# Experts' weight splits on VectorE in halves, narrowed pieces stored one piece later, float64 loads two ahead

## The chip, the core and the metric

The kernel runs on one core of a Trainium2 chip. A core has TensorE (PE in the profile; PEld is its weight load), VectorE (DVE), ScalarE (ACT), GpSimd (POOL) and SyncE (SP), which here issues most of the DMAs. Each engine works through its own queue in order and waits on semaphores for the others. The metric is the device time of one execution in microseconds, lower is better.

## The reference

Three stages follow each other, in float32.

```python
# attention: B=4, H=8, S=768, D=48
for t in range(S):
    cur = einsum('bhd,bhe->bhde', u[None] * kt, vt)
    y[:, :, t] = einsum('bhd,bhde->bhe', rt, state + cur)
    state = w[None, :, :, None] * state + einsum('bhd,bhe->bhde', kt, vt)
# experts: x of 3072 tokens x 384, 8 experts of 1024 hidden units, one expert for each token
expert_idx = argmax(x @ w_gate, axis=1)          # and its softmax weight gate_w
out[mask] = gate_w[mask, None] * (maximum(x[mask] @ w1[e], 0) @ w2[e])
# second layer: 2048 hidden units
h = x @ w_in
out = where(h > 0, h, exp(minimum(h, 0)) - 1) @ w_out
```

`w_in` and `w_out` of the second layer arrive as float64, since they are divided by a float64 scalar.

## The kernel before

**Attention** (`attention`, up to about 180 us) works in six chunks of 128 positions. In its last chunk the routing finds out which tokens go to which expert, and the first weights are already loaded and split.

**The experts' jobs.** `JOBS` lists nine jobs: the expert with the most tokens in two jobs of 256 slots (jobs 0 and 1), then the other seven with 448, 432, 416, 408, 408, 392 and 384 slots (jobs 2 to 8). A job has eight steps `f` of 128 hidden units. `step` gives TensorE a first group of nine matmuls (`layer1`, L757: three parts of 128 rows, and for each the products weight x data, weight x data rest, weight rest x data), which ends in `psl`; ScalarE makes `h` from it (L761) and VectorE the rest of `h` (L762). The second group (`layer2_columns`, L789, nine matmuls into `acc`) of a step comes LAG = 2 steps later, behind the first group of step f + 2. In steps 5 to 7 of a job `turn` transposes the next job's rows (L737), ScalarE copies them (L738) and VectorE takes the rest (L739, `xT`).

**The second layer** has six groups of 512 tokens (the code counts them as jobs 9 to 14) with 16 steps each: L757 again, then L766 on ScalarE, L767 and L768 on VectorE, L769 on ScalarE and L770 on VectorE, and twelve matmuls of 384 columns (L928). `take` (L747 on ScalarE, L748 on VectorE) splits the group's inputs. At the end GpSimd scatters the output rows.

**The weights** come in 40 chunks of 128 x 1536 float32 (768 KB): four for each of the eight experts, in their order, and eight for the second layer. `Stream.load` (L650) issues a load on SP's queue into `raw`, which has two buffers. `Stream.split` rounds it on ScalarE to a form that TensorE takes in one pass (L657, into one of four `wc` buffers; the last four chunks of the second layer have four buffers of their own) and subtracts that from the raw chunk (L659), on GpSimd except for chunks 2 and 3, which VectorE takes. `Stream.ahead` is called ahead of a step: at every even step it splits the chunk that is used two chunks later, and loads run one chunk ahead of the splits. A load waits for the subtraction that read its buffer last; the copy on ScalarE waits for its load and for the last matmuls that used its `wc` buffer.

**The narrowing** (`narrow_all`) turns the second layer's float64 weights, taken as bits, into float32 in DRAM (`w2f`), from where the last eight chunks are loaded. It is a generator with 16 pieces of 128 x 768: a load of 768 KB (`load_64`, L837, into `r64` with two buffers), five instructions on VectorE (L852, L855, L859, L862, L866) through the tiles `f` and `sg` with one buffer each, and a store of 384 KB on SP's queue (L867). It is called once in each step of jobs 1 to 8 and once more in steps 2, 4 and 6, eleven times a job, between `turn` and `step`; each call runs to the next `yield`, one instruction. `overflow_plan` (L962 to L1028) is spread over the steps of jobs 1 and 2 in the same way.

**GpSimd** also issues the gathers of the jobs' rows (L715, `xg`, two buffers) and the scatters of the slots (L67, `xi`).

The order of the instructions on each engine is that of the program (the schedule is written by hand). `order` (from L425) sorts the experts with small VectorE instructions.

Of the kernel before, what the change touches and what calls it, by code (L numbers as in the profile page):

```python
# [7 lines left out]
F32 = mybir.dt.float32  # L8
# [3 lines left out]
U32 = mybir.dt.uint32  # L12
ACTF = mybir.ActivationFunctionType
ALU = mybir.AluOpType
# [50 lines left out]
def scatter(tc, nc, apart, key, **kw):  # L65
    """no two scatters under one key write the same row"""
    ins = nc.gpsimd.indirect_dma_start(**kw).ins  # L67
    tc.declare_no_dep(ins, group=key, reason="rows of different tokens")
    tc.add_to_no_dep_group(key, ins)
    nc.gpsimd.memset(apart, 0.0)  # L70


def attention(tc, g, ctx, rkT, kv, wT, uT, wg):
    nc = tc.nc
    con = ctx.enter_context(tc.tile_pool(name="a_con", bufs=1))
    ld = ctx.enter_context(tc.tile_pool(name="a_ld", bufs=2))
    # what the last chunk no longer needs lies where weights will
    rk_b = [g.stream.wc.tile([128, 3, 2, B, C], F32, tag="wc", name=f"rkb{i}") for i in range(2)]
# [34 lines left out]
    def warm(n):  # L113
        """keeps the tensor engine's clock up where it would wait"""
        ps = p_m.tile([128, 512], F32, tag="m", name="psw")
        for _ in range(n):
            nc.tensor.matmul(ps, zero[:, 0:128], zero, start=True, stop=True, skip_group_check=True)
# [8 lines left out]

    # powers: ex[i] = w^(i-64), er[i] = w^(64-i); an inverse is taken at each power of two
    ex = con.tile([128, NP, 129], F32, name="ex")
# [9 lines left out]
    def grow(eng, up, down, step):  # L138
        """up[64 + j] and down[64 - j], j = 1 .. 64, from the powers step(i) = (2^i)-th"""
        for i in range(7):  # L140
            n = 1 << i
            m = min(n, 65 - n)
            for t, o, at in ((up, 64, 64 + n), (down, 65 - m, 65 - n - m)):
                if t is not None:
                    eng.tensor_tensor(out=t[:, :, at:at + m], in0=t[:, :, o:o + m],
                                      in1=step(i).to_broadcast([128, NP, m]), op=ALU.mult)

    nc.vector.tensor_copy(out=ex[:, :, 65:66], in_=w_sb.unsqueeze(2))
    for i in range(1, 7):
        n = 1 << i  # L150
# [45 lines left out]
    def pk_rows():  # L196
        """row form of the key powers, times w^128"""
        pks = wk.tile([128, NP, C], F32, tag="ot0", name="pks")
        nc.vector.tensor_tensor(out=pks, in0=pk, in1=w128.unsqueeze(2).to_broadcast([128, NP, C]), op=ALU.mult)
        ps = p_t.tile([128, NP, 128], F32, tag="t", name="pst")  # L200
        for p in range(NP):
            nc.tensor.transpose(ps[:, p, :], pks[:, p, :], g.ident)
        nc.scalar.copy(out=pkr, in_=ps.rearrange("s p (h d) -> s p h d", h=2)[:, :, :, 0:D])
# [22 lines left out]
    def state(c, q):  # L226
        """pairs 2q and 2q+1: the state at the start of chunk c + 1"""
        kr, v = kr_t[c], v_t[c]
# [110 lines left out]
    def rows(c, b, spare=False):  # L339
        """rows of x for a block of 128 tokens, times their gate: it is positive, so that relu lets it through"""  # L340
        if b == 0:
            x = xp.tile([128, B, ROW], F32, tag="x", name="x")
            nc.scalar.copy(out=x[:, :, TID], in_=tid[:, c, :])
            x_t[c] = x
        pool, tag = (p_m, "m") if spare else (p_t, "t")
        ps = pool.tile([128, NP, 128], F32, tag=tag, name="pst")
        for p in range(NP):
            nc.tensor.transpose(ps[:, p, :], o_t[c, p][:, b, :], g.ident)
        xv = x_t[c][:, b, 0:DM].rearrange("t (p h d) -> t p h d", p=NP, h=2)
        pv = ps.rearrange("t p (h d) -> t p h d", h=2)[:, :, :, 0:D]  # L350
        gate = gate_t[c][:, b:b + 1]
        nc.scalar.activation(out=xv, in_=pv, func=ACTF.Copy, scale=gate)
# [51 lines left out]
    def counts():  # L404
        """tells the experts apart by the tokens they have so far"""
        ps = p_m.tile([128, E], F32, tag="m", name="psc")
# [7 lines left out]
    def leader():  # L414
        """the expert with the most tokens of the first 2048: 256 or more, which fill the first job's slots"""
        key = counts()
# [7 lines left out]
    def order():  # L424
        """the experts after the leader, by the tokens they have so far"""  # L425
        key = counts()
# [14 lines left out]
    def place(c):  # L441
        """the rows in the order of the tokens, and each slot's row"""
        x, si = x_t[c], si_t.pop(c)
# [7 lines left out]
    def blank():  # L451
        """row 0 is what a slot without a token takes; its id is one that no scatter takes"""
        z = wk.tile([128, ROW], F32, tag="ot0", name="blank")
# [172 lines left out]
class Stream:  # L626
    """chunks of weights, 256 hidden units each: first the experts' in their order, then those of the second layer;
    split into a part that the tensor engine takes in one pass and the rest"""

# [9 lines left out]
    def which(self, p):  # L639
        """the expert at place p of the order"""  # L640
        if p not in self.expert:
# [12 lines left out]
    def split(self, i):  # L654
        w = self.pool(i).tile([128, 2, 1536], F32R, tag="wc", name="wc")
        r = self.loaded.pop(i)
        self.nc.scalar.copy(out=w[:, 0], in_=r)  # L657
        eng = self.nc.vector if i in (2, 3) else self.nc.gpsimd
        eng.tensor_tensor(out=w[:, 1], in0=r, in1=w[:, 0].bitcast(F32), op=ALU.subtract)  # L659
        self.ready[i] = w  # L660
        self.n_split = i + 1

    def ahead(self, n):
        """splits the chunks below n; loads run one ahead"""
        while self.n_split < min(n, self.n):
# [7 lines left out]
class Jobs:  # L673
    """the experts' slots in jobs of up to 512, then the second layer's tokens in groups of 512"""

# [25 lines left out]
    def load_i(self, u):  # L701
        """where the rows of the job's slots lie"""
        p, at, n = JOBS[u]
# [16 lines left out]
    def note(self, u):  # L720
        """the tokens of the job's slots, in the order that the second layer takes them in"""
        nc, g, (p, at, n) = self.nc, self.g, JOBS[u]
# [50 lines left out]
    def finish(self, u, k):  # L773
        """an expert's output to its columns; the next expert's overwrite those of empty slots"""
        nc, (p, at, n) = self.nc, JOBS[u]
# [37 lines left out]
def experts(tc, g, ctx, wpk2, out):  # L813
    nc = tc.nc
    stream, jobs = g.stream, g.jobs
    bp = ctx.enter_context(tc.tile_pool(name="m_b", bufs=1))
    # x of the second layer, columns in the order of the experts
    jobs.mid = mid = [bp.tile([128, N + WIDTH[1]], F32, name=f"mid{k}") for k in range(3)]
# [15 lines left out]
    def load_64(n):  # L834
        q, at = halves[n]
        r = dp.tile([128, 768], wpk2.dtype, tag="r64", name="r64", bufs=2)
        nc.sync.dma_start(out=r, in_=wpk2[0, q, :, at])  # L837
        return r

    def narrow_all():  # L840
        """float64 bits to the nearest float32, kept in DRAM for the second layer; one instruction at a time"""
        for _ in range(5):
            yield
        r = load_64(0)
        for _ in range(2):
            yield
        for n, (q, at) in enumerate(halves):
            v = r.bitcast(U32).rearrange("p (n t) -> p n t", t=2)
            lo, hi = v[:, :, 0], v[:, :, 1]
            r = load_64(n + 1) if n + 1 < len(halves) else None  # L850
            f = dp.tile([128, 768], U32, tag="f", name="f")
            nc.vector.tensor_scalar(out=f, in0=hi, scalar1=3, scalar2=0x3FFFFFF8, op0=ALU.logical_shift_left,  # L852
# [3 lines left out]
                                           op1=ALU.bitwise_or)  # L856
            yield
            t = dp.tile([128, 768], U32, tag="sg", name="sg")
            nc.vector.tensor_scalar(out=t, in0=f, scalar1=0xFF800000, scalar2=None, op0=ALU.bitwise_and)  # L859
# [6 lines left out]
            nc.vector.tensor_tensor(out=w, in0=w, in1=tail, op=ALU.add)  # L866
            nc.sync.dma_start(out=g.w2f[0, q, :, at], in_=w)  # L867
            yield

    narrowing = narrow_all() if wpk2.dtype != F32 else iter(())  # L870

    def clear():
        """columns that stay empty where an expert has more tokens than slots"""
        n = (N + WIDTH[1] - CAP) // 64
# [84 lines left out]
def overflow_plan(nc, g, pool, psum):  # L959
    """where each expert's tokens go between the layers; those beyond its slots, in items of 112 ranks"""  # L960
    cp = psum.tile([128, E], F32, tag="m", name="cp")
# [46 lines left out]
    yield  # L1008
    # each item's expert's width: the first's and the steps from there
    grow = pool.tile([128, E], F32, name="grow")  # L1010
# [20 lines left out]
def overflow(tc, g, wpk, out):  # L1031
    """both layers for the tokens beyond an expert's slots, one item after another"""
    nc = tc.nc
# [154 lines left out]
```

## Time and profile before

| | us |
|---|---|
| median of 3 runs (902.67 to 910.98) | 903.71 |
| span of the profiled execution, first to last instruction | 900.5 |
| TensorE busy in it | 803.0 |
| VectorE busy | 562.5 |
| ScalarE busy | 295.2 |
| GpSimd busy | 306.3 |

For the profiled execution the profile gives the span alone; the median of the runs is 3.2 us longer. The profile's numbers are of that one execution. A row of the timeline is: start, duration, engine, line, operation, output<-inputs, count, and in brackets the idle time of the engine just before and what ended it. A row of the waits is: who waited for whom, us in total, times, longest. A row of a group has the busy time and mean duration in ns, and then the idle time before. A row of one line's instructions has the shortest, median and longest duration in ns.

### The profile page before, as it was taken

How to read it: one execution, taken by the hardware profiler on the slowest of the kernel's cores; microseconds unless marked ns; L12 is line 12 of the kernel's file. 1: busy time of each engine (PE TensorE's matmuls, PEld its weight loads, DVE VectorE, ACT ScalarE, POOL GpSimd, SP SyncE). 2: the span in 40 equal slices, each digit the busy share in tenths (PEclk: the TensorE clock that was granted, in tenths of full speed). 3: DMA queues.
4: the chain of work that ended last, by engine and by line, in shares of the span. 5: the costliest groups of instructions: out<-in, count | busy, mean ns of one | idle time of the engine just before them, and what ended most of it. 6: DMA issues, size and time to landing. Idle time of an engine off the chain costs nothing. (4 is left out here: it accounts for less than half of the span.)

```text
span 900.5 us, 12702 instructions
## 1 busy us (share of the span) xinstructions
PE 803.0 (89%) x4960; PEld 708.1 (79%) x4962; DVE 562.5 (62%) x875; ACT 295.2 (33%) x485; POOL 306.3 (34%) x259
## 2 busy tenths in 40 slices
PE   6577877976879986999899999999999999999994
PEld 3455665766878985999897779999999999999993
DVE  8989999762586828686776774444444544444441
ACT  3111220243553432444344433333333333333221
POOL 7837337263365637375453331001001001001001
PEclk7879988998999989999999999999999999999998
DMA  9336563184876596597562200000000000001001
GB/s 347 126 129 107 169 153 42 40 158 96 197 188 155 214 198 174 153 254 164 197 211 93 101 1 22 15 1 27 10 0 30 7 1 36 1 1 36 1 0 38
DMA packets 31242, 87.54 MB, mean 97 GB/s; under 512 B 11582, under 2 KB 15182, under 8 KB 31178
## 3 DMA queue, kind: packets, MB, share of 16 engines
q1 hardware_dynamic: 26218, 76.57, 31.0%
q0 software_dynamic: 4672, 9.98, 4.4%
q8 instruction: 41, 0.67, 0.4%
q14 instruction: 23, 0.19, 0.1%
q10 hardware_dynamic: 288, 0.13, 0.1%
HBM read 70.67 MB, written 15.99 MB: 96 GB/s over the span
## 5 line engine op out<-in xcount | busy, mean ns | idle before, releaser
L757 PE MATMUL psl<-xT,wc 128*128 128x512 f32 (+6 forms) x1368 | 323.0, 380 | 8.7 <-DVE xT L739 8.7
L757 PEld LDWEIGHTS psl<-xT,wc 128*128 128x128 f32 x1368 | 254.9, 190 | 41.0 <-DVE xT L739 10.0
L928 PE MATMUL acc<-wc,h 128*128 128x384 f32 x1152 | 220.1, 338 | 4.0 <-ACT h L769 3.1
L928 PEld LDWEIGHTS acc<-wc,h 128*128 128x128 f32 x1152 | 204.1, 188 | 16.0 <-ACT h L769 5.7
L659 POOL TENSOR_TENSOR wc<-raw,wc 128x1536 fp32r<-128x1536 f32 x38 | 135.8, 3575 | 140.4 <-ACT wc L657 140.3
L67 POOL DMA_INDIRECT out_dram<-y,idT x24 | 24.7, 1031 | 331.8 <-ACT y L936 326.8
L789 PE MATMUL acc<-h,wc 128*128 128x408 f32 (+6 forms) x576 | 120.6, 352 | 13.4 <-DVE h L762 13.1
L767 DVE TENSOR_SCALAR ex<-ex 128x512 f32<-128x512 f32 x96 | 49.5, 516 | 125.3 <-ACT ex L766 125.3
L789 PEld LDWEIGHTS acc<-h,wc 128*128 128x128 f32 x576 | 104.7, 195 | 19.6 <-DVE h L762 17.6
L770 DVE TENSOR_TENSOR h<-ex,h 128x512 fp32r<-128x512 f32 x96 | 66.5, 693 | 65.9 <-ACT h L769 65.2
L769 ACT CAST h<-ex 128x512 fp32r<-128x512 f32 x96 | 59.6, 620 | 135.2 <-DVE ex L768 135.2
L766 ACT ACTIVATE ex<-psl 128x512 f32<-128x512 f32 x96 | 57.4, 597 | 131.3 <-PE psl L757 122.4
L657 ACT CAST wc<-raw 128x1536 fp32r<-128x1536 f32 x40 | 59.2, 1480 | 69.8 <-DMA raw<-in_wpk_dram 39.9
L768 DVE TENSOR_TENSOR ex<-ex,psl 128x512 f32<-128x512 f32 x96 | 66.0, 688 | 3.4
L852 DVE TENSOR_SCALAR f<-r 128x768 uint32<-128x768 uint32 x16 | 30.4, 1900 | 45.7 <-DMA w2f<-f 33.0
L761 ACT ACTIVATE h<-psl 128x408 fp32r<-128x408 f32 (+6 forms) x64 | 31.7, 499 | 58.3 <-PE psl L757 57.5
L67 POOL DMA_INDIRECT xi<-pos,si x24 | 25.9, 1080 | 71.4 <-DVE acc L401 67.1
L277 PE MATMUL psc<-rt,kt 64*128 64x128 f32 x384 | 34.5, 309 | 17.4 <-DVE a L287 15.1
L277 PEld LDWEIGHTS psc<-rt,kt 64*128 64x128 f32 x384 | 28.5, 207 | 26.8 <-DVE a L287 16.1
L762 DVE SCALAR_TENSOR_TENSOR h<-psl,h 128x408 fp32r<-128x408 f32 (+6 forms) x64 | 35.7, 559 | 21.3 <-ACT h L761 21.3
L315 ACT COPY ot<-pso 128x512 f32<-128x512 f32 x24 | 14.1, 586 | 88.3 <-PE pso L311 54.7
L169 DVE TENSOR_TENSOR kt<-rkb,er 128x512 f32<-128x512 f32 x14 | 41.5, 2972 | 0.3
(175 smaller groups left out, 798.2 us busy)
## 6 DMA issues: line engine op xcount, KB each, us to landing
raw<-in_wpk_dram SPq DMA_DIRECT2D x32, 768.0 KB
rkb<-in_rkT_dram SPq DMA_DIRECT2D x24, 512.0 KB
r<-in_wpk_dram SPq DMA_DIRECT2D x16, 768.0 KB
w2f<-f SPq DMA_DIRECT2D x16, 384.0 KB
raw<-w2f SPq DMA_DIRECT2D x8, 768.0 KB
xl<-x SPq DMA_DIRECT2D x6, 770.0 KB
v<-in_kv_dram SPq DMA_DIRECT2D x6, 768.0 KB
kb<-in_kv_dram SPq DMA_DIRECT2D x5, 768.0 KB
```

The costliest lines, as they stand in the source:

```text
L67: ins = nc.gpsimd.indirect_dma_start(**kw).ins
L277: nc.tensor.matmul(ps[hf][:, b, :], kt[r0:r0 + 64, b, :], rt[r0:r0 + 64, b, :], start=True, stop=True, skip_group_check=True)
L657: self.nc.scalar.copy(out=w[:, 0], in_=r)
L659: eng.tensor_tensor(out=w[:, 1], in0=r, in1=w[:, 0].bitcast(F32), op=ALU.subtract)
L757: nc.tensor.matmul(ps, self.w1(i, a, k, fi), xT[:, b, k], start=(m == 0), stop=(m == 8))
L766: nc.scalar.activation(out=ex, in_=ps, func=ACTF.Exp)
L767: nc.vector.tensor_scalar(out=ex, in0=ex, scalar1=1.0, scalar2=-1.0, op0=ALU.min, op1=ALU.add)
L768: nc.vector.tensor_tensor(out=ex, in0=ex, in1=ps, op=ALU.max)
L769: nc.scalar.copy(out=h[:, 0], in_=ex)
L770: nc.vector.tensor_tensor(out=h[:, 1], in0=ex, in1=h[:, 0].bitcast(F32), op=ALU.subtract)
L789: nc.tensor.matmul(self.acc[u][k], w[:, a, 128 * k:128 * k + 128], h[:, b], start=(f == 0 and m == 0), stop=(f == 7 and m == 2))
L928: nc.tensor.matmul(acc, h[:, a, 128 * j:128 * j + 128], jobs.w2(i, b, fi), start=(f == 0 and m == 0), stop=(f == 15 and m == 2))
```

## The change

All subtractions of `split` run on VectorE, each as two halves of 768 columns (the first holds the weights of the first group, the second those of the second). The narrowing has two buffers for `f`; the store of a piece is issued behind the second instruction of the next piece, and the last one at the end. `r64` has three buffers; two loads are issued at the start, two calls sooner than the first was, and then each piece issues the load of the piece two ahead. The first piece's first instruction stays at the same call. Comments and docstrings are removed.

```diff
@@ Stream.split
         self.nc.scalar.copy(out=w[:, 0], in_=r)
-        eng = self.nc.vector if i in (2, 3) else self.nc.gpsimd
-        eng.tensor_tensor(out=w[:, 1], in0=r, in1=w[:, 0].bitcast(F32), op=ALU.subtract)
+        for k in range(2):
+            at = slice(768 * k, 768 * k + 768)
+            self.nc.vector.tensor_tensor(out=w[:, 1, at], in0=r[:, at], in1=w[:, 0, at].bitcast(F32), op=ALU.subtract)
@@ load_64
-        r = dp.tile([128, 768], wpk2.dtype, tag="r64", name="r64", bufs=2)
+        r = dp.tile([128, 768], wpk2.dtype, tag="r64", name="r64", bufs=3)
@@ narrow_all
-        for _ in range(5):
+        for _ in range(3):
             yield
-        r = load_64(0)
-        for _ in range(2):
+        rs = [load_64(0), load_64(1)]
+        for _ in range(4):
             yield
+        done = None
         for n, (q, at) in enumerate(halves):
-            v = r.bitcast(U32).rearrange("p (n t) -> p n t", t=2)
+            v = rs.pop(0).bitcast(U32).rearrange("p (n t) -> p n t", t=2)
             lo, hi = v[:, :, 0], v[:, :, 1]
-            r = load_64(n + 1) if n + 1 < len(halves) else None
-            f = dp.tile([128, 768], U32, tag="f", name="f")
+            if n + 2 < len(halves):
+                rs.append(load_64(n + 2))
+            f = dp.tile([128, 768], U32, tag="f", name="f", bufs=2)
             nc.vector.tensor_scalar(out=f, in0=hi, scalar1=3, scalar2=0x3FFFFFF8, op0=ALU.logical_shift_left,
                                     op1=ALU.bitwise_and)
             yield
...
             yield
+            if done is not None:
+                nc.sync.dma_start(out=done[0], in_=done[1])
             t = dp.tile([128, 768], U32, tag="sg", name="sg")
...
             nc.vector.tensor_tensor(out=w, in0=w, in1=tail, op=ALU.add)
-            nc.sync.dma_start(out=g.w2f[0, q, :, at], in_=w)
+            done = g.w2f[0, q, :, at], w
             yield
+        nc.sync.dma_start(out=done[0], in_=done[1])
```

## The prediction

> **What bounds the kernel now.** The page's tenths show TensorE full from about 536 us on, with gaps before. So I cut out the experts' stage behind its two narrow jobs (247.2 us, job 2's first group, to 478.5, the second layer's first) and the start of the second layer, where the last weight chunks are still split, and read the busy time of each stretch (PE, PEld, DVE, ACT, POOL, granted clock, DMA share, GB/s).
>
> ```profile
> span 900.5 us, 12702 instructions
> 247.20:478.50 231.30, 209.19 (x1101) 198.90 (x1099) 161.98 (x182) 92.89 (x132) 130.74 (x53) 0.96 0.68 189
> 478.50:536.30 57.80, 53.85 (x252) 44.27 (x252) 41.09 (x42) 24.86 (x37) 21.04 (x6) 1.00 0.18 61
> ```
>
> In the first stretch PE is idle for 231.3 - 209.2 = 22.1 us. The view of waits for PE there has two lines, both name VectorE, and they cover 21.8 of it (us, times, longest).
>
> ```profile
> PE acc L789 <- DVE h L762: 13.1, 9, 3.6
> PE psl L757 <- DVE xT L739: 8.7, 3, 7.1
> ```
>
> What the stretches would take if PE never waited follows from undisturbed groups in the timeline. Nine matmuls of 408 columns come every 1.67 us, a step of two groups every 3.34, which is 8.19 ns per column and step.
>
> ```profile
> 391.58 1.84 PE L757 MATMUL psl<-xT,wc 128*128 128x408 f32 x9
> 393.26 1.82 PE L789 MATMUL acc<-h,wc 128*128 128x408 f32 x9
> 394.92 1.84 PE L757 MATMUL psl<-xT,wc 128*128 128x408 f32 x9
> ```
>
> A turn's transposes add 0.29 (303.12 - 302.83).
>
> ```profile
> 302.83 0.52 PE L737 MATMUL psq<-ident,xg 104*128 104x104 f32 x4
> 303.12 2.01 PE L757 MATMUL psl<-xT,wc 128*128 128x432 f32 x9
> ```
>
> The widths of jobs 2 to 8 add up to 2888; times 8 steps times 8.19 ns they give 189.2 us. With 18 turns (5.2) and two groups left of the 256-wide job (2.1) that is 196.5, against 231.3: **34.8 us are lost**, 22.1 as idle time and 12.7 as slow clock and ragged groups after it. In the second stretch 13 first groups of 512 columns and 11 second groups (12 matmuls of 384, the same columns) are 24 x 2.10 = 50.3 us, against 57.8: **7.5 us lost**. Together 42.3.
>
> Why VectorE is late, in the timeline (start, duration, what ended the idle time before):
>
> ```profile
> 322.40 0.56 DVE L852 TENSOR_SCALAR f<-r 128x768 uint32<-128x768 uint32 x1 [7.51 <-DMA w2f<-f]
> 323.53 3.25 PE L789 MATMUL acc<-h,wc 128*128 128x432 f32 x8 [3.40 <-DVE h L762]
> 326.58 3.24 PE L757 MATMUL psl<-xT,wc 128*128 128x416 f32 x9
> 353.96 4.67 DVE L852 TENSOR_SCALAR f<-r 128x768 uint32<-128x768 uint32 x1 [3.18 <-DMA w2f<-f]
> 354.77 3.42 POOL L659 TENSOR_TENSOR wc<-raw,wc 128x1536 fp32r<-128x1536 f32 x1
> 359.66 1.05 PE L757 MATMUL psl<-xT,wc 128*128 128x408 f32 x2 [7.08 <-DVE xT L739]
> 490.43 3.51 POOL L659 TENSOR_TENSOR wc<-raw,wc 128x1536 fp32r<-128x1536 f32 x1 [5.63 <-ACT wc L657]
> 490.88 3.34 DVE L767 TENSOR_SCALAR ex<-ex 128x512 f32<-128x512 f32 x1 [1.19 <-ACT ex L766]
> 496.24 0.42 DVE L767 TENSOR_SCALAR ex<-ex 128x512 f32<-128x512 f32 x1
> ```
>
> There are two causes. At 322.40 the narrowing's first instruction had waited 7.51 us for the store of the piece before, since `f` has one buffer; the `h` queued behind it came late. At 353.96 the same instruction, 0.56 us long elsewhere, lasts 4.67 and ends just after GpSimd's subtraction. At 490.88 a 0.42 us instruction lasts 3.34, again until that subtraction is over, with no store near: VectorE stands while GpSimd subtracts. And after the 3.40 us gap, 17 matmuls take 6.1 us that at full clock need 1.6 + 1.7, so 2.8 us more go.
>
> The Trainium skill (TensorE: Matmul & The Clock Gate, section What's actually happening) puts the fall to half clock behind an idle window of about 3.4 us. The 3.40 us gap agrees; by that page, shorter gaps would cost their own length alone.
>
> **The change, part by part.** *The subtractions.* GpSimd loses 38 of 3.5 us; VectorE runs 80 halves where it ran two whole ones. The rows are VectorE's whole subtraction, the narrowing's sum over 768 elements, the nearest row for a half (shortest 0.94, median 0.96), the subtractions in the first stretch (DVE, POOL), and the narrowing's five operations there.
>
> ```profile
> L659 DVE TENSOR_TENSOR wc<-raw,wc x2: 1759/1759/1759, 209.8 to 215.3; 128x1536 fp32r<-128x1536 f32 x2
> L866 DVE TENSOR_TENSOR f<-f,sg x16: 943/956/4658, 252.2 to 470.8; 128x768 f32<-128x768 f32 x16
> 247.20:478.50 231.30, 0.00 (x0) 101.07 (x29) 0.96 0.68 189
> L852 DVE TENSOR_SCALAR f<-r 128x768 uint32<-128x768 uint32 x15 | 29.8, 1990 | 45.7 <-DMA w2f<-f 33.0 <-issue 12.7
> L866 DVE TENSOR_TENSOR f<-f,sg 128x768 f32<-128x768 f32 x16 | 28.6, 1785 | 0.1
> L862 DVE SCALAR_TENSOR_TENSOR sg<-r,sg 128x768 f32<-128x768 uint32 x16 | 20.7, 1291 | 0.2
> L855 DVE SCALAR_TENSOR_TENSOR f<-r,f 128x768 uint32<-128x768 uint32 x16 | 18.0, 1126 | 0.1
> L859 DVE TENSOR_SCALAR sg<-f 128x768 uint32<-128x768 uint32 x16 | 14.7, 920 | 0.2
> ```
>
> A chunk costs VectorE between 1.76 (the whole) and 1.91 (two halves at 0.956); I take 1.9, so 29 chunks add 55.1 us. The five narrowing rows hold 111.8 us; unheld (0.55 for the two TENSOR_SCALAR, 0.95 for the others) they are 62.7, so 49.1 us of holding go. VectorE's busy time becomes 162.0 - 49.1 + 55.1 = 168.0 us, 85% of 196.5: nearly what it is, but nothing on it lasts over 1 us.
>
> What the added wait holds up: both halves wait for ScalarE's copy of their chunk, and behind them on VectorE stand the turn's subtraction, one or two narrowing instructions and the step's `h`. Count from the start of the copy, which waits for the last group that read its buffer:
>
> ```profile
> 299.53 1.48 ACT L657 CAST wc<-raw 128x1536 fp32r<-128x1536 f32 x1 [1.27 <-PE acc L789]
> ```
>
> The copy ends at 1.5, the halves at 3.4, two narrowing instructions at 5.3, `h` (0.6) at 5.9. PE wants this `h` two steps and a group later (LAG is 2): 2.5 x 3.53 = 8.8 at width 432. Some 2.9 us of slack hide the move; a copy later than that stops PE. In the second layer each step has a 0.42 (L767) and two of 0.69:
>
> ```profile
> L768 DVE TENSOR_TENSOR ex<-ex,psl 128x512 f32<-128x512 f32 x96 | 66.0, 688 | 3.4
> ```
>
> Two steps give VectorE 2 x (0.42 + 0.69 + 0.69) + 1.9 and at most 0.69 for a `take`, 6.2 of 8.4 us: it fits too.
>
> *Two `f`, the store one piece later.* The view of waits gives what goes (SP's queue, and VectorE):
>
> ```profile
> SPq L867 <- DVE f L866: 117.1, 16, 10.5
> DVE f L852 <- DMA w2f<-f: 33.0, 9, 7.5
> ```
>
> SP's timeline gives one store's issue:
>
> ```profile
> 313.90 0.33 SPq L867 DMA_DIRECT2D w2f<-f  x1
> ```
>
> A store issued at 313.90 had landed by 322.40, 8.5 us. With two buffers it has five narrowing calls, 5/11 of a job of 27 us or 12 us, so no wait is left. SP stands 117.1 us at the store's place, with the loads of raw weights queued behind; behind the next piece's second instruction it finds `f` finished, and the loads go out when their buffer is free. The issues are the same 16 stores and 16 float64 loads.
>
> *Float64 loads two ahead.* The narrowing's other wait (12.7 us, named issue) may be its load; a load gets one piece, 12 us, more. I price it at nothing: without it these waits stay, at most 2.8 us each, inside the slack. Three loads now go out at once near 228 us.
>
> GpSimd's gathers no longer queue behind subtractions: job 3's first went out at 247.65, behind one of them, and with two buffers the gathers of jobs 3 and 4 may both go out some 20 us sooner, beside those three loads.
>
> ```profile
> 247.65 1.68 POOL L715 DMA_INDIRECT xg<-xl,ix  x1 [0.18 <-DVE size L987]
> ```
>
> *The start.* Chunk 0's halves come ahead of the routing of attention chunk 4 on VectorE and wait for the first raw load (rows: VectorE's routing, the copy, VectorE's idle time after it, a held instruction of the order, and a later copy).
>
> ```profile
> 179.66 0.19 DVE L388 TENSOR_TENSOR sl<-psr,oh 128x32 f32<-128x32 f32 x1 [0.17 <-PE psr L385]
> 182.92 1.47 ACT L657 CAST wc<-raw 128x1536 fp32r<-128x1536 f32 x1 [5.54 <-DMA raw<-in_wpk_dram]
> 187.52 0.42 DVE L739 TENSOR_TENSOR xTe<-psq,xTe 128x256 fp32r<-128x256 f32 x1 [3.82 <-ACT xTe L738]
> 192.71 4.24 DVE L431 TENSOR_TENSOR sq<-key 128x64 f32<-128x64 f32 x1
> 208.31 1.47 ACT L657 CAST wc<-raw 128x1536 fp32r<-128x1536 f32 x1 [8.30 <-DMA raw<-in_wpk_dram]
> ```
>
> VectorE then goes on at 184.4 + 1.9 = 186.3 instead of 179.7, 6.6 us late. It was idle for 3.82 us before 187.52, and L431, another instruction that ends with a subtraction on GpSimd, gets shorter; but `order` itself waits for matmuls that wait for the late turns, so some 2 to 3 us of lateness reach the last scatters of slots and the gathers of job 1; the matmuls between hide in the 8.30 us wait for chunk 2. Bounds 0 to 3, I take 2 lost.
>
> **The sum**, in this execution's time: of 34.8 us I leave 7 (some 0.75 at each of six job changes, where gathers and loads meet, and 2.5 where the early gathers meet the three loads), so 27.8 come back; of 7.5 I leave 1; 2 are lost at the start: 27.8 + 6.5 - 2 = 32.3. The span becomes 868.2. The runs' median of 903.71 is 3.2 over the span, which I carry along: **871 us**. All back and nothing lost at the start gives 861.
>
> **The rivals.** *VectorE becomes the bound.* Each of 28 chunks makes it wait a copy's 1.5 us plus handing over 0.2 with nothing to do: 168 + 48 = 216 us for the stretch instead of 204. Then 15.3 + 6.5 - 2 = 19.8 come back: 884. For it: 85% of the time is taken, and in-order waits can't be filled with narrowing as now. Against: `h` of the next step can run until the copy is done. The Trainium skill (Perfetto Trace Analysis, section Optimizing Scalar/DVE Operations) advises moving work off a saturated VectorE, the opposite of this change, though it doubts that GpSimd is a help; the trace, with 3.3 us holds, shares the doubt.
>
> *One lateness for another.* VectorE's busy time hardly changes (162 to 168), and `h` is late as before: 900 to 908, no change. Against: its longest instruction falls from 4.67 to 1 us, which the slack covers.
>
> *Slower: late loads now stop VectorE too.* The stretch moves the same bytes in less time, the DMA share going from 0.68 to 0.68 x 231/204 = 0.77. A copy has waited 6.54 us for its load:
>
> ```profile
> 333.87 1.48 ACT L657 CAST wc<-raw 128x1536 fp32r<-128x1536 f32 x1 [6.54 <-DMA raw<-in_wpk_dram]
> ```
>
> At 6 us late, 3 beyond the slack, a chunk costs 3 of idle time and 1.5 of slow clock (about half the 2.8 after a 3.4 us gap). All 42.3 us, less 2, are eaten at nine such chunks; at twelve the time is 903.7 + 12 x 4.5 - 40.3 = 917. Against: the long waits came where SP stood at a store, and that ends.
>
> **Chances.** Forecast 0.68 (861 to 878), VectorE the bound 0.16 (878 to 890), no change 0.07, slower 0.09. The first two hold 0.84, so the range is theirs, with 3 us below for what else may shift: 858 to 890. A measurement of this kernel tells about 1% (9 us) from no change; faster by more than that 0.84, within 0.07, slower 0.09.
>
> **What would show it.** Right: no GpSimd subtraction, L767 at 0.42 throughout, halves near 0.95, L852 without a wait for its store, SP not standing at the store, PE's two waits for VectorE down from 21.8 to under 6 us, job 2 to 478.5 shortened to about 204 us. Wrong: PE waits for `h` behind a half that waited for a copy (a bound VectorE, or late loads by what the copy waited for), or job 1 starting later than 232 us.

## The result, and the profile after

The changed kernel takes 875.44 us (median of 4, 873.54 to 878.47) against 907.35 us for the kernel before (median of 4, 902.67 to 915.41) measured beside it; the ratio is 0.968, 95% interval 0.962 to 0.974. The forecast was 871, in a range of 858 to 890. Its profiled execution has a span of 874.8 us, against 900.5.

The stretches of the prediction, cut at the same groups (columns: length, then busy time of PE, PEld, DVE, ACT, POOL, granted clock, DMA share, GB/s). Job 1 is in front of them this time, since it changed too.

```profile
span 874.8 us, 12765 instructions
230.10:250.38 20.28, 17.88 (x140) 17.46 (x139) 7.87 (x26) 8.81 (x16) 8.50 (x8) 0.94 0.88 196
250.38:459.61 209.23, 201.89 (x1100) 195.92 (x1099) 155.53 (x241) 95.88 (x137) 19.95 (x16) 0.98 0.76 210
459.61:510.59 50.98, 50.91 (x251) 44.95 (x251) 35.98 (x56) 25.25 (x38) 0.00 (x0) 1.00 0.19 66
```

Jobs 2 to 8 went from 231.3 to 209.2 us, the start of the second layer from 57.8 to 51.0, and job 1 from 17.8 (229.40 to 247.20) to 20.3. VectorE's busy time fell from 162.0 to 155.5 although it took over 58 half subtractions. The groups of VectorE, from 250.38 to 459.61, say why (busy, mean ns, idle time before):

```profile
L660 DVE TENSOR_TENSOR wc<-raw,wc 128x768 fp32r<-128x768 f32 x58 | 53.0, 955 | 50.0 <-ACT wc L657 45.9 <-issue 2.4 <-PE psl L758 1.5
L872 DVE TENSOR_TENSOR f<-f,sg 128x768 f32<-128x768 f32 x16 | 15.2, 952 | 0.1
L855 DVE TENSOR_SCALAR f<-r 128x768 uint32<-128x768 uint32 x15 | 8.3, 552 | 0.0
```

The store's wait of L852 (now L855) is gone, and the narrowing's instructions are at the unheld lengths: 0.552 where the mean was 1.990, 0.952 where it was 1.785. In the second layer the line that had lasted 3.34 us at 490.88 (now L768) never exceeds 0.43. PE waits for little, and SyncE's queue waits for little at the store (waits of PE from 250.38 to 459.61, then SyncE's two rows for the store and for the halves):

```profile
L768 DVE TENSOR_SCALAR ex<-ex x96: 417/428/429, 464.1 to 854.4; 128x512 f32<-128x512 f32 x96
PE psl L758 <- ACT xT L739: 5.2, 1, 5.2
PE psl L758 <- DVE xT L740: 2.2, 2, 1.3
SPq L863 <- DVE f L872: 7.8, 8, 2.4
SPq L650 <- DVE wc L660: 117.5, 26, 8.5
```

SyncE stood 117.1 us at the store's place before and stands 7.8 there now. In all it stands hardly less (the sum of its waits is 190 us before and 178 now), since it now waits longer at the loads of raw weights, for the halves that free their buffer (the last row). Before, that wait was for GpSimd's subtractions, and shorter:

```profile
SPq L650 <- POOL wc L659: 59.9, 18, 5.1
```

At L650 a load waits for its own buffer; at the store, loads whose buffers may have been free waited behind another engine's result.

What is left of the loss lies at one place. This is SyncE's queue around job 1, before and then after (start, duration):

```profile
225.13 1.44 SPq L650 DMA_DIRECT2D raw<-in_wpk_dram  x2
228.30 2.06 SPq L837 DMA_DIRECT2D r<-in_wpk_dram  x2
242.92 0.34 SPq L650 DMA_DIRECT2D raw<-in_wpk_dram  x1
```

```profile
229.65 0.34 SPq L650 DMA_DIRECT2D raw<-in_wpk_dram  x1
230.29 5.97 SPq L838 DMA_DIRECT2D r<-in_wpk_dram  x2
236.47 0.86 SPq L650 DMA_DIRECT2D raw<-in_wpk_dram  x1
237.37 0.87 SPq L838 DMA_DIRECT2D r<-in_wpk_dram  x1
```

Before, the weights of chunks 4 and 5 (`raw`) were asked for together, ahead of the float64 loads (`r`). Now the float64 loads are issued two calls sooner: they stand between the two chunks, and a third follows at once. The gathers of jobs 3 and 4 go out in the same microseconds:

```profile
230.11 1.07 POOL L716 DMA_INDIRECT xg<-xl,ix  x1 [1.40 <-PE acc L790]
240.88 1.06 POOL L716 DMA_INDIRECT xg<-xl,ix  x1 [1.51 <-DMA xe<-xl,ix]
```

These are the first and the last of eight; before, the first came at 247.65. Chunk 5, asked for at 236.47, was there at 254.36, and TensorE paid for it:

```profile
254.36 1.47 ACT L657 CAST wc<-raw 128x1536 fp32r<-128x1536 f32 x1 [9.27 <-DMA raw<-in_wpk_dram]
250.38 0.78 PE L758 MATMUL psl<-xT,wc 128*128 128x448 f32 x3
256.32 0.71 PE L758 MATMUL psl<-xT,wc 128*128 128x448 f32 x1 [5.16 <-ACT xT L739]
263.52 3.41 PE L758 MATMUL psl<-xT,wc 128*128 128x448 f32 x9
267.83 1.96 PE L758 MATMUL psl<-xT,wc 128*128 128x448 f32 x9
```

ScalarE is in order, so the copy that waited for the load kept back the cast of `xT` behind it. From 250.38 to 267.83 two groups of 256 and two of 448 columns ran; at 8.19 ns for a column of two groups that is 5.8 us of work, so some 11.7 are lost, with job 1's 2.5 before them. From 267.83 to 459.61 PE is busy for the whole of it:

```profile
267.83:459.61 191.78, 191.78 (x1064) 187.76 (x1063) 144.30 (x218) 88.37 (x126) 19.95 (x16) 1.00 0.75 212
```

### The profile page after: what moved, and what is told of

The parts are those of the page before. It is cut to its first block, busy times and chain, and to the rows that moved or that the text cites. A ratio compares the mean times of both kernels' runs of the same rounds, so it can differ in the third digit from the quotient of the medians.

```text
span 874.8 us, 12765 instructions
## 1 busy us (share of the span) xinstructions
PE 795.7 (91%) x4962; PEld 707.8 (81%) x4962; DVE 547.5 (63%) x953; ACT 294.6 (34%) x485; POOL 169.6 (19%) x221
## 5 line engine op out<-in xcount | busy, mean ns | idle before, releaser
L935 PE MATMUL acc<-wc,h 128*128 128x384 f32 x1152 | 217.9, 337 | 0.1
L768 DVE TENSOR_SCALAR ex<-ex 128x512 f32<-128x512 f32 x96 | 41.0, 427 | 124.8 <-ACT ex L767 124.8
L790 PE MATMUL acc<-h,wc 128*128 128x408 f32 (+6 forms) x576 | 114.3, 343 | 2.4 <-DVE h L763 1.6
L660 DVE TENSOR_TENSOR wc<-raw,wc 128x768 fp32r<-128x768 f32 x80 | 73.1, 955 | 63.3 <-ACT wc L657 59.2
L716 POOL DMA_INDIRECT xg<-xl,ix x24 | 28.4, 1185 | 127.7 <-DMA idl<-xg 96.2
L277 PE MATMUL psc<-rt,kt 64*128 64x128 f32 x384 | 32.8, 301 | 14.1 <-DVE a L287 12.7
```

The lines of the kernel that those rows point to most:

```text
L277: nc.tensor.matmul(ps[hf][:, b, :], kt[r0:r0 + 64, b, :], rt[r0:r0 + 64, b, :], start=True, stop=True, skip_group_check=True)
L660: self.nc.vector.tensor_tensor(out=w[:, 1, at], in0=r[:, at], in1=w[:, 0, at].bitcast(F32), op=ALU.subtract)
L790: nc.tensor.matmul(self.acc[u][k], w[:, a, 128 * k:128 * k + 128], h[:, b], start=(f == 0 and m == 0), stop=(f == 7 and m == 2))
L935: nc.tensor.matmul(acc, h[:, a, 128 * j:128 * j + 128], jobs.w2(i, b, fi), start=(f == 0 and m == 0), stop=(f == 15 and m == 2))
```

## The experiments

Times are medians, and each ratio is to the kernel before measured beside it: 907.02 us for the two parts alone, loads one ahead and gathers held; 908.73 for changed again, two `f` only, GpSimd busy and both; 903.3 for the other four. The other columns are of the one profiled execution of each: where job 1 begins, its length, jobs 2 to 8, and the start of the second layer, which runs as in the prediction from its first group to its fourteenth first group.

| kernel | us | ratio, 95% | job 1 at | job 1 | jobs 2-8 | 2nd layer |
|---|---|---|---|---|---|---|
| before | 907.35 | | 229.4 | 17.8 | 231.3 | 57.8 |
| changed | 875.44 | 0.962-0.974 | 230.1 | 20.3 | 209.2 | 51.0 |
| changed, again | 877.57 | 0.960-0.970 | 232.8 | 24.7 | 204.4 | 51.1 |
| subtractions only | 894.86 | 0.981-0.991 | 233.4 | 24.2 | 219.9 | 51.2 |
| narrowing only | 881.92 | 0.967-0.976 | 231.6 | 17.9 | 209.0 | 57.8 |
| two `f` only | 898.02 | 0.982-0.992 | 230.6 | 23.5 | 224.2 | 57.8 |
| two `f`, store later | 876.29 | 0.963-0.975 | 229.5 | 17.9 | 205.3 | 57.8 |
| halves in 2nd layer only | 870.79 | 0.956-0.967 | 229.4 | 18.1 | 206.4 | 51.0 |
| changed, GpSimd busy | 903.57 | 0.991-0.998 | 226.6 | 21.5 | 237.4 | 51.0 |
| changed, loads one ahead | 873.57 | 0.960-0.969 | 229.4 | 18.0 | 201.3 | 51.0 |
| changed, gathers held | 876.01 | 0.962-0.971 | 225.5 | 19.9 | 204.1 | 51.1 |
| changed, both | 866.96 | 0.950-0.962 | 225.7 | 19.3 | 200.6 | 51.0 |
| changed, both, again | 870.30 | 0.955-0.967 | 234.2 | 20.2 | 200.0 | 51.1 |
| changed, whole subtractions | 878.12 | 0.965-0.976 | 231.5 | 25.8 | 204.1 | 51.0 |

### The two parts alone

The subtractions alone: the kernel before with

```diff
-        eng = self.nc.vector if i in (2, 3) else self.nc.gpsimd
-        eng.tensor_tensor(out=w[:, 1], in0=r, in1=w[:, 0].bitcast(F32), op=ALU.subtract)
+        for k in range(2):
+            at = slice(768 * k, 768 * k + 768)
+            self.nc.vector.tensor_tensor(out=w[:, 1, at], in0=r[:, at], in1=w[:, 0, at].bitcast(F32), op=ALU.subtract)
```

> Only the subtractions move to VectorE in halves; the narrowing is that of before. Theory (both causes of the prediction count): no VectorE instruction is held any more, so the second layer's start gets its 6.8 us back in full (51.0 us from the first group to the 14th, as with the whole change), but VectorE still waits for the store of the piece before, so the stretch of jobs 2 to 8 gets back only about half of its 22 us: 883 to 892 us. Rival (the holding was all): within 2 us of the whole change. Rival (the store wait was the main thing): over 895.

Measured 894.86 (890.75 to 896.48), between the theory's range and the second rival's 895. The second layer's start came down to 51.2; jobs 1 to 8 (24.2 + 219.9) gained 5.0 of 249.1. The stores stayed in the way: SyncE stood longer at them than the 117.1 us of before, while VectorE's wait for them came down from 33.0 us (waits of SyncE's queue and of VectorE in jobs 2 to 8):

```profile
SPq L868 <- DVE f L867: 140.1, 16, 13.6
DVE f L853 <- DMA w2f<-f: 14.7, 7, 2.8
```

The narrowing alone is the changed kernel with that edit undone.

> Only the narrowing changes (two f, store one piece later, float64 loads two ahead); the subtractions stay on GpSimd. Theory: the 33 us of waiting for stores go, the 49 us of holding stay and so do the 57.8 us of the second layer's start: 888 to 899 us, PE still waiting 8 to 15 us for VectorE in jobs 2 to 8. Rival (the holding costs nothing once f has two buffers): under 884.

Measured 881.92: the theory missed, and the rival's "under 884" held. Jobs 2 to 8 took 209.0 us, as in the first profile of the whole change, with GpSimd's 29 subtractions still beside them: VectorE was busy for 185.3 of the 209.0, held as before, and PE waited for it for 7.1 us. From job 4 to the end of job 8, behind the loss at jobs 1 to 3, they took 143.1 us against the whole change's 139.5, so the holding cost some 3.6 there. The second layer's start stayed at 57.8. So an account in which both causes share the 34.8 us by their microseconds on VectorE fell here.

### The store: VectorE's wait, or SyncE's

The kernel before, with one argument more:

```diff
-            f = dp.tile([128, 768], U32, tag="f", name="f")
+            f = dp.tile([128, 768], U32, tag="f", name="f", bufs=2)
```

> The kernel before with only this: the narrowed piece f has two buffers. The store stays where it was, SyncE still stands at it, and the float64 loads and the GpSimd subtractions are untouched. Theory 3 (what cost was VectorE standing at the store of the piece before): most of the narrowing part's 25 us comes, time 881 to 889. Rival (what cost was SyncE standing at the store with the weights' loads behind it): little comes, 897 to 906.

Measured 898.02, in the rival's range. VectorE no longer waits for a store, and that is worth 7 us of jobs 2 to 8 (224.2; this execution lost 5.7 in job 1, and with 901.99 us it was the longest of the four). Of what is left, much shows at ScalarE (waits in jobs 2 to 8):

```profile
SPq L867 <- DVE f L866: 89.5, 15, 10.4
ACT wc L657 <- DMA raw<-in_wpk_dram: 72.6, 17, 12.5
```

The copies wait 72.6 us for their weights, which stood behind SyncE at the store; in the kernel before it is 26.1. Then, on top of the two `f`, the store's place, with loads one ahead as before:

```diff
+        done = None
...
+            if done is not None:
+                nc.sync.dma_start(out=done[0], in_=done[1])
             t = dp.tile([128, 768], U32, tag="sg", name="sg")
...
-            nc.sync.dma_start(out=g.w2f[0, q, :, at], in_=w)
+            done = g.w2f[0, q, :, at], w
...
+        nc.sync.dma_start(out=done[0], in_=done[1])
```

> The kernel before with two f and the store one piece later, float64 loads one ahead as before, GpSimd still subtracting. Against the kernel with two f alone (898) only the store's place on SyncE's queue differs; against the narrowing part alone (882) only the float64 loads. Theory 3 as it stands now (two f alone moved jobs 2 to 8 from 231 to 224 us, the rest of the narrowing part's 22 is SyncE no longer standing at the store): jobs 2 to 8 in 206 to 212 us, time 878 to 886. Rival (the second float64 load ahead brings the rest): jobs 2 to 8 at 220 us or more, time 893 to 899.

Measured 876.29, a little under the theory: as much as the whole change. Jobs 2 to 8 took 205.3 us, and the same two rows became:

```profile
SPq L862 <- DVE f L871: 2.3, 5, 0.5
ACT wc L657 <- DMA raw<-in_wpk_dram: 26.0, 11, 4.5
```

So of the 26 us between 231.3 and 205.3, taking VectorE's own wait away first brings some 7, and then SyncE's standing at the store 19; by the medians, 10.7 and 16.3. The other order was not run (with one `f` the next piece needs the buffer that the store still reads), so these are not shares of two independent costs. The second float64 load ahead has no part in them.

### Where the holding costs

The changed kernel, with GpSimd's subtractions back for the experts' chunks and the halves for the second layer's alone:

```diff
+        if i < 4 * E:
+            eng = self.nc.vector if i in (2, 3) else self.nc.gpsimd
+            eng.tensor_tensor(out=w[:, 1], in0=r, in1=w[:, 0].bitcast(F32), op=ALU.subtract)
-        for k in range(2):
+        for k in range(2 if i >= 4 * E else 0):
```

> The changed kernel with the experts' chunks (all but the second and third of the first expert) subtracted by GpSimd again, whole, and VectorE's halves only for the eight chunks of the second layer. Theory 2 as it stands now (the holding costs where VectorE has little room, and with the narrowing part in place it has room in jobs 2 to 8; it costs 6.8 us in the start of the second layer): the start of the second layer in 51 us, jobs 2 to 8 in 205 to 212, time 873 to 878, no different from the whole change. Rival (the holding costs in jobs 2 to 8 too, and the whole change hides that gain behind its own loss at the meeting of gathers and loads): 879 to 884, with waits of PE for VectorE of over 10 us.

Measured 870.79, rather below the whole change than above it. Eight chunks' halves bring the second layer's 6.8 us (57.8 to 51.0); those of the other chunks brought nothing: from job 4 to the end of job 8 this kernel and the whole change both take 139.47 us. (With loads one ahead as well it was not run.) Then the changed kernel with a GpSimd subtraction added for each chunk split in the experts' stage, whose result nobody reads:

```diff
+        if self.idle is not None:
+            self.nc.gpsimd.tensor_tensor(out=self.idle, in0=w[:, 0].bitcast(F32), in1=w[:, 0].bitcast(F32), op=ALU.subtract)
...
+    stream.idle = dp.tile([128, 1536], F32, tag="idle", name="idle")
```

> The changed kernel with one more GpSimd subtraction of 1536 columns for each chunk split in the experts' stage, into a tile that nobody reads: VectorE is held beside it as before the change, and no work waits for it. Theory 2 (from the narrowing alone, whose jobs 2 to 8 took 209.0 us, no longer than the whole change's 209.2): without the store's wait the holding costs next to nothing in jobs 2 to 8; time within 4 us of the changed kernel, 873 to 880. Rival (the prediction's own account, in which the holding is over half of the waits for VectorE): half of the 34.8 us comes back as loss; 886 to 893.

Measured 903.57 (899.0 to 916.6): the theory missed, and the rival's 886 to 893 too, by over 10 us. Jobs 2 to 8 and the halves in them:

```profile
248.18:485.62 237.44, 210.87 (x1100) 197.46 (x1099) 223.24 (x242) 93.83 (x132) 116.06 (x53) 0.96 0.67 182
L661 DVE TENSOR_TENSOR wc<-raw,wc 128x768 fp32r<-128x768 f32 x58 | 89.5, 1582 | 9.8 <-ACT wc L658 9.8
PE acc L793 <- DVE h L766: 17.6, 10, 5.8
```

The halves take 1582 ns instead of 955, VectorE is busy for 223 of 237 us, and PE waits for `h`. That is the prediction's first rival, VectorE as the bound, made to happen. Both runs together say what neither says alone: the holding costs nothing or little where VectorE has room (from job 4 on, none with the halves in the second layer only, and some 3.6 us in the narrowing alone, at 185.3 of 209.0 us for jobs 2 to 8), and 28 us of jobs 2 to 8 where it has none (237.4 against 209.2). The Trainium skill (SBUF — State Buffer, section Who interferes with whom) calls the port that both engines share an exclusive lock; the lengthened halves agree with it.

### The loss at jobs 1 and 2

The changed kernel a second time:

> The changed kernel once more, for a second profile. Theory 1: the 14 us that its first profile lost between the start of job 1 and the middle of job 2 (2.5 us in job 1, 11.8 in the 17.5 us after it) come from the meeting of early gathers and float64 loads, which is in the program: then the second profile loses them again, within 3 us, and the median is 873 to 878. Rival: the meeting is a matter of how the transfers fall in one execution: then the second profile's jobs 1 to 8 differ from the first's 229.5 us by over 5 us, and the single times spread over more than 5 us.

Measured 877.57, and both halves of the question got an answer: jobs 1 to 8 took 229.1 us (first 229.5), but now job 1 lost more (24.7) and jobs 2 to 8 less (204.4). The loss comes back with the program; where in it the loss falls does not. Then three variants. Loads one ahead puts the float64 loads back where they were:

```diff
-        r = dp.tile([128, 768], wpk2.dtype, tag="r64", name="r64", bufs=3)
+        r = dp.tile([128, 768], wpk2.dtype, tag="r64", name="r64", bufs=2)
...
-        for _ in range(3):
+        for _ in range(5):
             yield
-        rs = [load_64(0), load_64(1)]
-        for _ in range(4):
+        rs = [load_64(0)]
+        for _ in range(2):
...
-            if n + 2 < len(halves):
-                rs.append(load_64(n + 2))
+            if n + 1 < len(halves):
+                rs.append(load_64(n + 1))
```

> The whole change, but float64 loads one ahead as before (two buffers, first load two calls later). Theory A (the jam at 230 to 267 us is made by the third float64 load in SP's queue ahead of the raw loads): job 2 starts without its long gap, 865 to 870 us. Theory B (it is made by the gathers of jobs 3 and 4, which GpSimd now sends at 230 to 241 us): as the whole change, 873 to 878. In both the stretch from job 3 on stays free of PE waits, since the load two ahead was priced at nothing.

Gathers held puts a one-element copy ahead of the gathers, which waits for a subtraction of the job before:

```diff
             if 1 < u < NJ - 1 and f == 0:
+                nc.gpsimd.tensor_copy(out=g.apart, in_=stream.ready[jobs.chunk(u, 0) + 1][0:1, 1, 1535:1536].bitcast(F32))
                 jobs.load_x(u + 1)
```

> The whole change, with a one-element copy on GpSimd ahead of each job's gathers that waits for the last subtraction of the job before, so that the gathers go out about when they did before. Theory B (gathers make the jam): the copy of chunk 6 waits under 3 us for its load instead of 9.3, job 2's start loses under 4 us instead of 11.8, 863 to 869 us. Theory A (third float64 load): 873 to 878.

Measured 873.57 and 876.01, and either alone is undecided. Their profiled executions, 865.57 and 867.08 us, were the fastest of each, and the others ran from 873.49 to 877.05 and from 871.51 to 878.02; what those lost no profile shows. With both edits:

> The changed kernel with float64 loads one ahead (two buffers) and with the gathers of jobs 3 and on held by a one-element GpSimd copy until the last subtraction of the chunk before. Theory 1 (the loss at jobs 1 and 2 needs the gathers and the float64 loads together, and either alone still costs in some executions): all times at 864 to 869, 8 us below the changed kernel's in this call. Rival (the loss has nothing to do with either; the two profiles at 864 were lucky executions): median 872 to 878, no different from the changed kernel, with single times spread over 865 to 878.

Measured 866.96, single times 863.05 to 871.55: a wider spread than the theory's 864 to 869, but all below the changed kernel's 875.25 to 879.66 beside it. And once more, in the last series:

> Once more the changed kernel with float64 loads one ahead and the gathers held. Theory 1: 863 to 872 again, 8 us or more below the changed kernel's 873 to 880. Rival (the first time was a lucky chip): 873 to 878.

Measured 870.30. SyncE's queue is in the old order (its rows, the copy of chunk 5, and jobs 2 to 8 of the first of the two):

```profile
225.41 1.43 SPq L650 DMA_DIRECT2D raw<-in_wpk_dram  x2
226.97 1.71 SPq L838 DMA_DIRECT2D r<-in_wpk_dram  x2
240.24 1.48 ACT L657 CAST wc<-raw 128x1536 fp32r<-128x1536 f32 x1 [0.79 <-DMA raw<-in_wpk_dram]
244.97:445.60 200.63, 198.35 (x1101) 193.01 (x1099) 153.54 (x239) 92.79 (x132) 29.44 (x30) 1.00 0.80 219
```

Chunk 5 is copied at 240.24, and jobs 1 to 8 take 219.9 and 220.2 us, against the changed kernel's 229.5 and 229.1: the meeting of early float64 loads and early gathers costs 9.3 us. This version takes 0.950 to 0.962 of the time before in the one series and 0.955 to 0.967 in the other; the changed kernel was measured beside it in the first alone.

### Halves or wholes

The changed kernel with one subtraction of 1536 columns per chunk.

> The changed kernel with one subtraction of 1536 columns per chunk on VectorE instead of two of 768. Theory (a half took 0.954 us, so two cost 1.91 against 1.76 for a whole; both are far from what VectorE can't fit): time within 3 us of the changed kernel's 875 to 878, VectorE's busy time 5 us lower, PE's waits for h no longer. Rival (an instruction of 1.76 us ahead of h eats the slack of 2.9 us): PE waits for h at several chunks, 882 to 890.

Measured 878.12, no different. VectorE's busy time in jobs 2 to 8 is 153.4 against 155.3 in the changed kernel's second execution, 2 us lower and not 5, since two halves one behind the other take 1.83 us together. PE never waits for `h` in its profile, so the halves buy nothing here.

## Why the prediction was right, and where it was not

The time held: 875.44 against 871. Its two large terms came out as 28.9 us instead of 34.3 in the profiled execution, and the reasons are mixed. The saving is 31.9 us by the medians and 25.7 by the two profiled executions, where the sum had 32.3; that the medians come so near it is in part luck, with single times before from 902.67 to 915.41.

**The start of the second layer**, 6.5 expected: 57.8 to 51.0, so 6.8. The ten kernels without GpSimd's subtractions there have 51.0 to 51.2, the four with them 57.8. Before, PE's only waits there, 3.1 us, were for ScalarE's `h`, which follows the held line on VectorE, and none was for weights: shown, mechanism and size.

**Jobs 2 to 8**, 27.8 expected: 22.1, with 2.5 more lost in job 1. The term that failed is the 2.5 us "where the early gathers meet the three loads", and beside it the float64 loads two ahead that were priced "at nothing": the meeting measures 9.3 us. I had the three loads and the early gathers in the text, but did not lay out SyncE's queue: two float64 loads moved past the weights of chunk 5, and those came 12 us later than before (copied at 254.36 instead of 242.40); not all of that is the overtaking, since chunk 4's load, ahead of them in the queue, went out 4.5 us later as well (229.65 instead of 225.13). Without the meeting jobs 1 to 8 take 220 us, 29 less than before, where the prediction had 27.8 plus its 2.5. The 0.75 us at each of six job changes come near as a sum (200.6 us is 4.1 over the 196.5, and six times 0.75 is 4.5), but not where they were put: 3.2 of the 4.1 lie in jobs 2 and 3, which take 30.5 and 30.7 us where the prediction's rates give 28.7 and 29.3.

**The two causes** in these jobs were seen, but sized by VectorE's time, which is not what they cost; the sum did not show it, since the change takes both away. Of VectorE's lost time the prediction put 49.1 us to the holding and 33.0 to the store, and the other wait of 12.7 us perhaps to the float64 load. But two `f` and the store's place, with the holding left in, give 26 us of 34.8, and the subtractions alone 5 in jobs 1 to 8. The 12.7 us were not the load: with two `f` alone, and the loads as before, L852 waits for nothing. With the store moved, VectorE has room in which the holding disappears; with the holding gone, SyncE still stands. The weightier cost of the store, taken in the order that was run, was not VectorE's wait (7 us) but SyncE's standing there (19 us), whose 117.1 us the prediction quoted and gave no price.

**The start of job 1**, 2 lost, can't be resolved: the same program began it at 225.7 and at 234.2 us. The kernels that subtract the first chunks on VectorE begin it at 225.5 to 234.2, those that do so on GpSimd at 229.4 to 231.6. The changed kernel's second execution began it at 232.8, past the 232 that the prediction named as a sign of being wrong.

**The rivals.** VectorE did not become the bound (155.5 of 209.2 us, where the sum had 168), but it does once something holds it again (903.57). The idle wait for the copies that this rival counted, 48 us, is there (50.0 before the halves), but TensorE waits for almost none of it. One lateness for another fell, with waits for VectorE at 2.2 us in jobs 2 to 8. Late loads, the slower case, did appear, at one place only, and through ScalarE, whose waiting copy kept back `xT`: the price of some 9 us is about two of that rival's chunks.

**Not settled:** how much of the 9.3 us belongs to the loads' order and how much to the gathers, since either edit alone gave mixed times. The profiles narrow it. Jobs 1 and 2 together take 60.2 to 61.0 us where both are early (changed twice, whole subtractions), 53.5 to 55.0 with early loads and late gathers (gathers held, narrowing alone, halves in the second layer only), and 49.8 to 50.5 with neither and the store out of the way (both twice, and two `f` with the store later); GpSimd busy is left aside. So early loads cost some 4 us without the gathers, and some 6 come with them (job 3 gives 1 back). What early gathers cost without early loads stays open: jobs 1 and 2 took 50.1 us in one profile (loads one ahead), but 61.0 in another (subtractions only, with the stores in the way as in the kernel before, which took 54.6).

## What to carry to other kernels

A queue that stands at a store for an engine's result holds every load behind it; price the loads that could have gone out meanwhile, not only the wait that the store causes on an engine. A load that waits at the head for its own buffer is another matter: that standing grew here, and the time fell. When loads are moved earlier, write down the order of the queue before and after: what they overtake is late by their transfer. Two causes of one engine's lateness don't add: take one away, then ask whether the engine has room, before paying for the second.

## What the runs showed of the hardware

TensorE stood in job 1 with nothing to wait for that the profile shows: 4.5 us in the changed kernel's second execution, 4.9 with whole subtractions, 3.9 with the subtractions only. These rows are of the first of the three, with the DMA share of the same microseconds (0.85, then 1.01):

```profile
243.01 0.28 PE L758 MATMUL psl<-xTe,wc 128*128 128x256 f32 x1 [1.71 <-issue]
244.42 0.37 PE L758 MATMUL psl<-xTe,wc 128*128 128x256 f32 x1 [1.14 <-issue]
245.82 0.57 PE L758 MATMUL psl<-xTe,wc 128*128 128x256 f32 x1 [1.03 <-issue]
240.00:245.00 5.00, 1.58 (x9) 0.98 (x7) 0.00 (x0) 0.00 (x0) 2.18 (x3) 0.95 0.85 238
245.00:250.00 5.00, 3.97 (x17) 3.69 (x18) 1.31 (x3) 2.36 (x4) 1.01 (x1) 0.50 1.01 274
q8 instruction: 41, 0.67, 0.4%
```

The last row is a queue that the profile names "instruction": 41 packets, 0.67 MB. One of its packets fell at 244.15 in this execution, in the middle of the gaps. But the two executions with both edits, which have no such gap, have one in job 1 too (at 236.66 and 245.94). That TensorE's instructions themselves came late is therefore a guess, and not shown.

A short gap can cost the clock. In the kernel with both edits TensorE idled for 1.71 us and soon after ran at a granted clock of 0.50, 27 matmuls of 256 columns taking 6.61 us where the prediction's rate gives 3.1:

```profile
223.66 0.55 PE L738 MATMUL psq<-ident,xe 128*128 128x128 f32 x3 [1.71 <-DMA xe<-xl,ix]
225.66 6.61 PE L758 MATMUL psl<-xTe,wc 128*128 128x256 f32 x27
225.60:231.00 5.40, 5.28 (x23) 4.82 (x22) 1.26 (x5) 3.85 (x9) 0.27 (x1) 0.50 0.90 34
```

The Trainium skill (TensorE: Matmul & The Clock Gate, section What's actually happening) lets the clock fall after an idle window of about 3.4 us; here a gap of half that was followed by 5.4 us at half clock, and the nearest longer one, 5.16 us, had ended 14 us before it. The measurement decides: the prediction's reading of that page, by which shorter gaps would cost their own length alone, does not hold here.
